# Second product of an FFN as seven products of half blocks in place of eight, after attention, on one core

## Chip, core and metric

One core of a Trainium2 chip. The metric is the device time of one execution in microseconds (us). The kernel before takes 512.01 us (median of 3 runs, 511.5 to 512.92). Positions in the timeline are counted from the start of the profiler's span of one execution. PE is the matrix engine (PEld its loading of weights), DVE the vector engine, ACT the scalar engine, POOL the engine that issues the loads.

## Reference

Attention with projected keys and values (8 batches, 8 heads, 1024 tokens, head size 64), then a feed-forward network (FFN) whose hidden values are squared:

```python
k_proj, v_proj = einsum('ks,bhsd->bhkd', E, k), einsum('ks,bhsd->bhkd', F, v)
x = softmax(q @ k_proj.T / 8) @ v_proj        # heads joined: 8192 x 512
h = maximum(x @ w_in, 0.0)                    # 8192 x 2048
out = (h * h) @ w_out                         # 8192 x 512
```

## The kernel before

Each batch is cut into two chunks of 512 tokens. A chunk is 16 steps of the first product, then its second product. Attention for the next batch is put between these steps by hand (the `plan`).

```python
def square(self, c, fb, ps):                  # after each block of the first product
    r = relu_pool.tile([P, TCH], BF16, name="h_relu")
    nc.scalar.activation(r[:], ps[:], AF.Relu)
    nc.vector.tensor_tensor(out=self.hsq[c][:, fb, :], in0=r[:], in1=r[:], op=ALU.mult)

def first_mm(self, c, fb, cb, ps):            # 64 per chunk, 128x512
    nc.tensor.matmul(ps[:], lhsT=w_in_blk(cb, fb), rhs=..., ...)

def second_mm(self, c, tb, fb, ps, m=slice(0, DM)):    # 4 token blocks x 16 = 64 per chunk, 128x512
    nc.tensor.matmul(ps[:, m], lhsT=self.hsq[c][:, fb, tb * P:(tb + 1) * P], rhs=w_out_blk(fb)[:, m], ...)
...
with tc.manual_schedule(engines={PE}):        # only PE runs in the order of this text
    ...
    att.project_v(V_PIECES[0])
    ...
    for b in range(B):
        if b == 0:
            at(1, att.project_v, V_PIECES[1])           # PE, then a cast of vp on DVE
            at(2, att.chunk_values, 0, 1, (0,))         # PE reads vp; then xT on DVE
            at(2, att.project_v, V_PIECES[2])
            at(3, att.chunk_values, 0, 1, (1,))
            ...
```

Each engine but PE gets its order when the kernel is built, not from the text.

The softmax here doesn't subtract the row's maximum and nothing guards it: scores larger than these inputs give would overflow.

Of the kernel before, what the change touches and what calls it, by code (L numbers as in the profile page):

```python
# [8 lines left out]
P = 128  # L9
F32 = mybir.dt.float32  # L10
BF16 = mybir.dt.bfloat16
AF = mybir.ActivationFunctionType
ALU = mybir.AluOpType
# [5 lines left out]
def kernel(  # L19
# [11 lines left out]
    nc = tc.nc  # L31

    B, H, S, D = q.shape
# [3 lines left out]
    DM = moe_w_out.shape[1]  # L37
    assert D == 64 and KP == 64 and C == CM == 512 and S == 1024 and H == 8
    NI = 8
# [9 lines left out]


    out_rows = out.rearrange("(b p i) m -> b i p m", p=P, i=NI)

    const_pool = ctx.enter_context(tc.tile_pool(name="const", bufs=1))
    wpool = ctx.enter_context(tc.tile_pool(name="wpool", bufs=1))
    qkv_pool = ctx.enter_context(tc.tile_pool(name="qkv", bufs=2))
    proj_pool = ctx.enter_context(tc.tile_pool(name="proj", bufs=2))
    qt_pool = ctx.enter_context(tc.tile_pool(name="qt", bufs=2))
    soft_pool = ctx.enter_context(tc.tile_pool(name="soft", bufs=3))
    x_pool = ctx.enter_context(tc.tile_pool(name="x", bufs=2))
    relu_pool = ctx.enter_context(tc.tile_pool(name="relu", bufs=8))  # L60
    hsq_pool = ctx.enter_context(tc.tile_pool(name="hsq", bufs=2))
    out_pool = ctx.enter_context(tc.tile_pool(name="outp", bufs=4))
    aps = ctx.enter_context(tc.tile_pool(name="aps", bufs=2, space=bass.MemoryType.PSUM))
    fps = ctx.enter_context(tc.tile_pool(name="fps", bufs=4, space=bass.MemoryType.PSUM))
# [4 lines left out]
    def bank(shape=(P, 512), dtype=F32):  # L69
        return fps.tile(list(shape), dtype, tag="bank", name="ps_bank")  # L70
# [53 lines left out]
    for j in range(WP):  # L124
        if j == WP - 1:
            load(Q0[:, :, 4:8, :], tokens(q, 0, i=slice(4, 8)))
        t = wpool.tile([P, fn, DM], BF16, name=f"w_out_{j}")
        load(t[:], w_out_view[:, j * fn:(j + 1) * fn, :])
        w_out_sb.append(t)

    def w_in_blk(cb, fb):
        t, j = w_in_at[fb]
# [2 lines left out]
    def w_out_blk(fb):  # L135
        return w_out_sb[fb // fn][:, fb % fn, :]
# [214 lines left out]
    class Ffn:  # L351
# [6 lines left out]
        def square(self, c, fb, ps):  # L358
            r = relu_pool.tile([P, TCH], BF16, name="h_relu")
            nc.scalar.activation(r[:], ps[:], AF.Relu)  # L360
            nc.vector.tensor_tensor(out=self.hsq[c][:, fb, :], in0=r[:], in1=r[:], op=ALU.mult)  # L361

        def first_mm(self, c, fb, cb, ps):
            nc.tensor.matmul(  # L364
# [3 lines left out]

        def second_mm(self, c, tb, fb, ps, m=slice(0, DM)):
            nc.tensor.matmul(  # L370
                ps[:, m], lhsT=self.hsq[c][:, fb, tb * P:(tb + 1) * P], rhs=w_out_blk(fb)[:, m],
                start=(fb == 0), stop=(fb == NFB - 1),
            )

# [5 lines left out]

        def steps(self):
            for c in range(2):
                self.hsq[c] = hsq_pool.tile([P, NFB, TCH], BF16, name="hsq")
                first = self.cold and c == 0
                fb0 = 0
                if first:

                    banks = [bank() for _ in range(4)]
                    for cbs, fbs in (
                        ((0, 1), (0, 1)), ((0, 1), (2, 3)), ((2,), (0, 1)), ((2,), (2, 3)), ((3,), (0, 1, 2, 3)),  # L390
                    ):
                        for fb in fbs:
                            for cb in cbs:
                                self.first_mm(c, fb, cb, banks[fb])
                            if cbs[-1] == NCB - 1:
                                self.square(c, fb, banks[fb])
                        if (cbs, fbs) != ((2,), (2, 3)):
                            yield
                    fb0 = 4
                for fb in range(fb0, NFB):  # L400
                    ps = bank()
                    for cb in range(NCB):
                        self.first_mm(c, fb, cb, ps)
                    self.square(c, fb, ps)
                    yield
                if first:

                    for t0 in range(0, 4, 2):
                        banks = [bank() for _ in range(2)]
                        for j in range(WP):  # L410
                            for t in range(2):
                                for fb in range(j * fn, (j + 1) * fn):
                                    self.second_mm(c, t0 + t, fb, banks[t])
                                if j == WP - 1:
                                    self.store(c, t0 + t, banks[t])
                                yield
                else:
                    last = self.b == B - 1 and c == 1
                    for tb in range(4):
                        if last and tb == 3:  # L420

                            for m in (slice(0, DM // 2), slice(DM // 2, DM)):
                                ps = bank()
                                for fb in range(NFB):
                                    self.second_mm(c, tb, fb, ps, m)
                                self.store(c, tb, ps, m)
                            break
                        ps = bank()
                        for j in range(WP):
                            for fb in range(j * fn, (j + 1) * fn):  # L430
                                self.second_mm(c, tb, fb, ps)
                            if j == WP - 1:
                                self.store(c, tb, ps)
                            yield

    with tc.manual_schedule(engines={PE}):
# [29 lines left out]
        for b in range(B):  # L466
            plan = {}

            def at(step, fn, *args, **kwargs):
                plan.setdefault(step, []).append(lambda: fn(*args, **kwargs))  # L470

            if b == 0:
                at(1, att.project_v, V_PIECES[1])
                at(2, att.chunk_values, 0, 1, (0,))
                at(2, att.project_v, V_PIECES[2])
                at(3, att.chunk_values, 0, 1, (1,))
                at(21, att.transpose_q_chunk, 1, Q0, 0)
                at(21, att.transpose_q_chunk, 1, Q0, 1)
                at(23, att.chunk_scores, 1, 0)
                at(23, att.chunk_scores, 1, 1)  # L480
                at(25, att.sums, 0)
                at(27, att.chunk_values, 1, 0)
                at(27, att.chunk_values, 1, 1)
                nxt = Attention(1)
                nxt.load()
            if b + 1 < B:
                if b + 2 < B:
                    coming = Attention(b + 2)
                    coming.load()
                if b == 0:  # L490
                    at(36, nxt.project)
                    at(39, nxt.transpose_q, 0)
                    at(39, nxt.transpose_q, 1)
                    at(39, nxt.transpose_k)
                    at(41, nxt.scores, 0)
                    at(41, nxt.scores, 1)
                    at(44, nxt.transpose_q, 2)
                    at(44, nxt.transpose_q, 3)
                    at(45, nxt.sums, 0)
                    at(48, nxt.values, 0, True)  # L500
                    at(48, nxt.scores, 2)
                    at(51, nxt.values, 1)
                    at(51, nxt.scores, 3)
                    at(55, nxt.sums, 2)
                    at(55, nxt.values, 2)
                    at(55, nxt.values, 3, True)
                else:
                    at(14, nxt.scores, 0)
                    at(14, nxt.scores, 1)
                    at(18, nxt.sums, 0)  # L510
                    at(18, nxt.values, 0, True)
                    at(18, nxt.scores, 2)
                    at(27, nxt.values, 1)
                    at(27, nxt.scores, 3)
                    at(49, nxt.sums, 2)
                    at(49, nxt.values, 2)
                    at(49, nxt.values, 3, True)
                if b + 2 < B:
                    if b == 0:
                        at(61, coming.project)  # L520
                        at(63, coming.transpose_q_dma)
                        at(64, coming.transpose_k)
                    else:
                        at(27, coming.project)
                        at(30, coming.transpose_q_dma)
                        at(29, coming.transpose_k_dma)
            for step, _ in enumerate(Ffn(att, b == 0).steps(), 1):
                for stage in plan.pop(step, []):
                    stage()
            assert not plan, plan  # L530
            att, nxt = nxt, coming
# [30 lines left out]
```

## Time and profile before

| | before |
|---|---|
| time, us | 512.01 |
| PE busy | 97% |
| a batch in the steady part (first chunk + second chunk), us | 31.80 + 28.63 = 60.43 |
| first chunk of the last batch, without attention, us | 27.63 |
| start of the second batch's FFN, us | 90.35 |

The head of the profile page: busy time of each engine, its share of the span, and its instructions.

```profile
span 511.2 us, 6930 instructions
...
PE 498.3 (97%) x2727; PEld 223.3 (44%) x2778; DVE 217.0 (42%) x438; ACT 273.2 (53%) x412; POOL 33.0 (6%) x45
...
PEclk9999999999999999999999999999999999999999
```

PE is busy throughout, at full clock (a 9 stands for 90% or more). The view of PE's waits (who waited for whom: total us, times, longest; `issue` means for nothing that the profile shows) has nothing large:

```profile
PE ps_bank L370 <- issue: 2.9, 18, 0.2
PE ps_bank L151 <- DVE zeros L107: 1.2, 1, 1.2
PE ps_bank L364 <- ACT o_sb L377: 1.1, 2, 0.8
...
```

The timeline of PE (start us, us, line, result and operands, shape, count; in brackets the idle time before and what ended it). L364 is the first product, L370 the second:

```profile
212.65 1.89 PE L364 MATMUL ps_bank<-xT,w_in_115 128*128 128x512 bf16 x8
...
244.45 1.89 PE L364 MATMUL ps_bank<-xT,w_in_115 128*128 128x512 bf16 x8
...
273.08 1.24 PE L364 MATMUL ps_bank<-xT,w_in_115 128*128 128x512 bf16 x5
...
452.52 1.89 PE L364 MATMUL ps_bank<-xT,w_in_115 128*128 128x512 bf16 x8
...
480.15 1.03 PE L364 MATMUL ps_bank<-xT,w_in_115 128*128 128x512 bf16 x4
...
502.59 1.03 PE L370 MATMUL ps_bank<-w_out_131,hsq 128*128 128x512 bf16 x4
503.46 1.03 PE L370 MATMUL ps_bank<-w_out_134,hsq 128*128 128x512 bf16 x4
504.32 0.60 PE L370 MATMUL ps_bank<-w_out_127,hsq 128*128 128x256 bf16 x4
504.76 0.60 PE L370 MATMUL ps_bank<-w_out_129,hsq 128*128 128x256 bf16 x4
```

The first five lines are the starts of chunks: three of the steady part give 31.80 and 28.63 us, and the two of the last batch 27.63 us. The others give the price of a matmul from start to start: 0.863 us for four of 512 columns, 215.8 ns each, and 0.4375 us for four of 256, 109.4 ns each. Durations overlap, so starts are to be read, not durations.

Last, the same view for PE in the start (L211 projects v, L272 uses the result `vp`, L364 is the FFN):

```profile
19.85 0.64 PE L211 MATMUL ps_att<-V_sb,FT 128*64 128x128 bf16 x16
20.52 1.04 PE L364 MATMUL ps_bank<-xT,w_in_118 128*128 128x512 bf16 x4
21.49 0.30 PE L272 MATMUL ps_att<-expT,vp 64*64 64x256 bf16 x4
21.78 0.64 PE L211 MATMUL ps_att<-V_sb,FT 128*64 128x128 bf16 x16
```

### The profile page before, as it was taken

How to read it: one execution, taken by the hardware profiler on the slowest of the kernel's cores; microseconds unless marked ns; L12 is line 12 of the kernel's file. 1: busy time of each engine (PE TensorE's matmuls, PEld its weight loads, DVE VectorE, ACT ScalarE, POOL GpSimd, SP SyncE). 2: the span in 40 equal slices, each digit the busy share in tenths (PEclk: the TensorE clock that was granted, in tenths of full speed). 3: DMA queues.
4: the chain of work that ended last, by engine and by line, in shares of the span. 5: the costliest groups of instructions: out<-in, count | busy, mean ns of one | idle time of the engine just before them, and what ended most of it. 6: DMA issues, size and time to landing. Idle time of an engine off the chain costs nothing.

```text
span 511.2 us, 6930 instructions
## 1 busy us (share of the span) xinstructions
PE 498.3 (97%) x2727; PEld 223.3 (44%) x2778; DVE 217.0 (42%) x438; ACT 273.2 (53%) x412; POOL 33.0 (6%) x45
## 2 busy tenths in 40 slices
PE   8899999999999999999999999999999999999997
PEld 4344444444444444444444444444444444444444
DVE  2453766444434445345352354434443443522130
ACT  2464584664717556375654837366472755544351
POOL 7420100121000020001000000000000000000000
PEclk9999999999999999999999999999999999999999
DMA  9999999899997199204931060100102011010102
GB/s 179 204 205 223 225 207 205 129 232 181 185 203 157 42 176 206 82 0 115 184 82 44 1 161 16 61 22 32 62 1 81 2 42 42 23 61 21 63 0 82
DMA packets 67872, 54.18 MB, mean 106 GB/s; under 512 B 29184, under 2 KB 59392, under 8 KB 67840
## 3 DMA queue, kind: packets, MB, share of 16 engines
q0 software_dynamic: 30640, 29.23, 36.3%
q1 hardware_dynamic: 37200, 24.52, 18.0%
q8 instruction: 21, 0.34, 0.3%
q14 instruction: 11, 0.09, 0.1%
HBM read 59.24 MB, written 16.78 MB: 149 GB/s over the span
## 4 chain that ended last, share of the span: by engine, by line
PE 85%; DMA 9%; issue 2%; ACT 2%; POOL 1%; DVE 1%; SPq 0%; POOLq 0%; ACTq 0%
PE ps_bank L364 40%; PE ps_bank L370 38%; DMA w_out_134<-in_moe_w_out_dram 4%; DMA V_sb<-in_v_dram 3%; PE ps_bank L191 2%; DMA out_dram<-o_sb 2%; PE ps_att L262 1%; PE ps_att L296 1%; PE ps_att L318 1%; PE ps_bank L318 1%; DVE rs L306 1%; ACT rs L301 0%; ACT rs L300 0%; PE ps_bank L247 0%; ACT expT L276 0%
## 5 line engine op out<-in xcount | busy, mean ns | idle before, releaser
L361 DVE TENSOR_TENSOR hsq<-h_relu 128x512 bf16<-128x512 bf16 x256 | 108.9, 425 | 192.9 <-ACT h_relu L360 191.8
L360 ACT ACTIVATE h_relu<-ps_bank 128x512 bf16<-128x512 f32 x256 | 151.3, 599 | 69.7 <-PE ps_bank L364 69.6
L370 PEld LDWEIGHTS <-hsq 128*128 128x128 bf16 x1040 | 99.7, 98 | 123.5 <-issue 9.3
L377 ACT COPY o_sb<-ps_bank 128x512 f32<-128x512 f32 (+1 forms) x65 | 37.7, 580 | 121.2 <-PE ps_bank L370 111.4
L370 PE MATMUL ps_bank<-w_out_127,hsq 128*128 128x512 bf16 (+1 forms) x257 | 65.6, 376 | 0.2
L370 PE MATMUL ps_bank<-w_out_134,hsq 128*128 128x512 bf16 (+1 forms) x251 | 64.1, 376 | 1.6 <-issue 1.1
L370 PE MATMUL ps_bank<-w_out_131,hsq 128*128 128x512 bf16 (+1 forms) x252 | 64.3, 376 | 1.1 <-issue 1.0
L370 PE MATMUL ps_bank<-w_out_129,hsq 128*128 128x512 bf16 (+1 forms) x249 | 64.2, 376 | 1.1 <-issue 0.8
L306 DVE COPY rs<-rs 32x1024 f32<-32x1024 f32 x60 | 41.6, 693 | 47.0 <-ACT rs L301 46.0
L364 PE MATMUL ps_bank<-xT,w_in_125 128*128 128x512 bf16 x255 | 59.0, 379 | 0.1
L364 PE MATMUL ps_bank<-xT,w_in_121 128*128 128x512 bf16 x250 | 57.7, 379 | 0.4
L364 PE MATMUL ps_bank<-xT,w_in_123 128*128 128x512 bf16 x247 | 57.4, 379 | 0.4
L276 ACT ACTIVATE expT<-ps_att 128x1024 bf16<-128x1024 f32 x32 | 31.8, 1023 | 18.0 <-PE ps_att L262 18.0
L364 PEld LDWEIGHTS <-w_in_123 128*128 128x128 bf16 x256 | 25.0, 98 | 30.4 <-issue 0.4
L364 PEld LDWEIGHTS <-w_in_121 128*128 128x128 bf16 x256 | 24.9, 98 | 30.3 <-issue 0.7
L364 PEld LDWEIGHTS <-w_in_125 128*128 128x128 bf16 x256 | 24.4, 98 | 31.0 <-issue 2.7
L364 PE MATMUL ps_bank<-xT,w_in_115 128*128 128x512 bf16 x128 | 30.9, 379 | 1.1 <-DVE xT L347 1.1
L364 PE MATMUL ps_bank<-xT,w_in_118 128*128 128x512 bf16 x126 | 30.3, 379 | 1.3 <-ACT o_sb L377 1.1
L300 ACT ACTIVATE rs<-ps_att 128x1024 f32<-128x1024 f32 x15 | 15.4, 1024 | 12.7 <-PE ps_att L296 12.7
L322 DVE TENSOR_TENSOR xT<-ps_att,rs 128x512 bf16<-128x512 f32 x28 | 18.1, 686 | 8.8 <-PE ps_att L318 8.5
L364 PEld LDWEIGHTS <-w_in_115 128*128 128x128 bf16 x128 | 12.5, 98 | 16.5 <-issue 2.3
L364 PEld LDWEIGHTS <-w_in_118 128*128 128x128 bf16 x128 | 12.3, 98 | 16.4 <-issue 1.7
(72 smaller groups left out, 237.1 us busy)
## 6 DMA issues: line engine op xcount, KB each, us to landing
out_dram<-o_sb SPq DMA_DIRECT2D x63, 256.0 KB, 2.0
K_sb<-in_k_dram POOLq DMA_DIRECT2D x7, 1024.0 KB, 22.1
V_sb<-in_v_dram POOLq DMA_DIRECT2D x7, 1024.0 KB, 26.8
Q_sb<-in_q_dram POOLq DMA_DIRECT2D x7, 1024.0 KB, 14.8
k_f_93<-in_k_dram SPq DMA_DIRECT2D x1, 512.0 KB, 4.2
Q_sb<-in_q_dram POOLq DMA_DIRECT2D x2, 256.0 KB, 7.2
K_sb<-in_k_dram POOLq DMA_DIRECT2D x1, 512.0 KB, 7.9
V_sb<-in_v_dram POOLq DMA_DIRECT2D x1, 512.0 KB, 10.1
```

The source lines that it names most:

```text
L191: nc.tensor.matmul(ps[LO, :], lhsT=ET[:, i, :], rhs=self.K[:, :, i, :], start=f, stop=l)
L262: nc.tensor.matmul(ps[o, par], lhsT=self.kT[r, h % 4, h // 4, :], rhs=self.qT[r, h, n, :], start=True, stop=True)
L276: nc.scalar.activation(e[:], ps[:], AF.Exp, scale=SCALE)
L300: nc.scalar.activation(rs[1][:], ps[:], AF.Ln)
L306: nc.vector.tensor_copy(rs[j][lack:lack + 32], rs[j][have:have + 32])
L318: nc.tensor.matmul(ps_x[par][o], lhsT=self.vp[r, 2 * pr + a, :], rhs=e[r, par], start=True, stop=True)
L322: nc.vector.tensor_tensor(out=self.xT[:, pr, :, par], in0=ps_x[par].rearrange("p (c t) -> p c t", c=2), in1=rs[:, par].rearrange("p (c t) ...
L360: nc.scalar.activation(r[:], ps[:], AF.Relu)
L361: nc.vector.tensor_tensor(out=self.hsq[c][:, fb, :], in0=r[:], in1=r[:], op=ALU.mult)
L364: nc.tensor.matmul(ps[:], lhsT=w_in_blk(cb, fb), rhs=self.xT[:, cb, c].rearrange("p a t -> p (a t)"), start=(cb == 0), stop=(cb == NCB - 1),)
L370: nc.tensor.matmul(ps[:, m], lhsT=self.hsq[c][:, fb, tb * P:(tb + 1) * P], rhs=w_out_blk(fb)[:, m], start=(fb == 0), stop=(fb == NFB - 1),)
L377: nc.scalar.copy(o[:, m], ps[:, m])
```

## The change

It cuts a chunk's h into quarters (two halves of tokens, two of the hidden size) and w_out likewise, and forms the product of two 2x2 block matrices with seven block products in place of eight (a scheme after Strassen and Winograd). The price is sums of quarters: of h once per chunk, of w_out once. It is used from the second batch on. Pools shrink to make room. Two smaller parts are not shown below: the last token block is no longer split into halves of 256 columns, and some attention steps no longer use spare banks.

```diff
-    qt_pool = ctx.enter_context(tc.tile_pool(name="qt", bufs=2))
+    qt_pool = ctx.enter_context(tc.tile_pool(name="qt", bufs=1))
-    relu_pool = ctx.enter_context(tc.tile_pool(name="relu", bufs=8))
+    relu_pool = ctx.enter_context(tc.tile_pool(name="relu", bufs=4))
...
+    w_sum = wpool.tile([P, 4, HF, HM], BF16, name="w_sum")
+    def sum_w_out():                          # 8 DVE instructions, 128x1024 bf16
+        for j in range(2):
+            ...
+            for o, x, y in ((t1, b12, b11), (t3, b22, b12), (t2, b22, t1), (t4, b21, t2)):
+                nc.vector.tensor_tensor(out=o, in0=x, in1=y, op=ALU.subtract)
...
+        def sum_h(self, c, f):                # 4 DVE instructions, twice per chunk
+            ...
+        def half_product(self, c, n, i, ps, fresh):
+            h = self.h_form(c, n)
+            for fb in range(HF):              # 8 matmuls, 128x256
+                nc.tensor.matmul(ps[:, i * HM:(i + 1) * HM], lhsT=h[:, fb, i * P:(i + 1) * P],
+                                 rhs=w_out_form(n, fb), ...)
...
+        def seven_products(self, c):
+            first, chain, other = bank(), bank(), bank()
+            half(c, 1, 0, first, True)
+            yield
+            half(c, 1, 1, first, True)
+            nc.scalar.copy(chain[:], first[:])
+            ...                               # 5, 6, 2, 7, 2, 4, 3; chain copied out to u after 6 and 7
...
-                for fb in range(fb0, NFB):
+                order = [fb for j in range(HF) for fb in (j, HF + j)] if seven else range(fb0, NFB)
+                for n, fb in enumerate(order):
...
-                    at(18, nxt.scores, 2)
+                    at(21, nxt.scores, 2)     # and 27 -> 26, 49 -> 48, 49 -> 51 for other steps
...
                     if b == 0:
                         at(61, coming.project)
                         at(63, coming.transpose_q_dma)
                         at(64, coming.transpose_k)
+                        at(64, sum_w_out)     # the last step of the first batch
```

More of the change, by code (lines that the diff above doesn't have):

```diff
@@ L51 @@
     out_rows = out.rearrange("(b p i) m -> b i p m", p=P, i=NI)
+    out_tokens = out.rearrange("(b p i) m -> b p i m", p=P, i=NI)
+    HF, HM = NFB // 2, DM // 2
     const_pool = ctx.enter_context(tc.tile_pool(name="const", bufs=1))
@@ L56 @@
     proj_pool = ctx.enter_context(tc.tile_pool(name="proj", bufs=2))
-    qt_pool = ctx.enter_context(tc.tile_pool(name="qt", bufs=2))
+    qt_pool = ctx.enter_context(tc.tile_pool(name="qt", bufs=1))
     soft_pool = ctx.enter_context(tc.tile_pool(name="soft", bufs=3))
     x_pool = ctx.enter_context(tc.tile_pool(name="x", bufs=2))
-    relu_pool = ctx.enter_context(tc.tile_pool(name="relu", bufs=8))
+    relu_pool = ctx.enter_context(tc.tile_pool(name="relu", bufs=4))
     hsq_pool = ctx.enter_context(tc.tile_pool(name="hsq", bufs=2))
+    form_pool = ctx.enter_context(tc.tile_pool(name="form", bufs=1))
+    part_pool = ctx.enter_context(tc.tile_pool(name="part", bufs=2))
     out_pool = ctx.enter_context(tc.tile_pool(name="outp", bufs=4))
@@ L129, with w_out_form @@
         w_out_sb.append(t)
+    w_sum = wpool.tile([P, 4, HF, HM], BF16, name="w_sum")
+    def sum_w_out():
+        for j in range(2):
+            f = slice(j * fn, (j + 1) * fn)
+            t1, t2, t3, t4 = (w_sum[:, n, f] for n in range(4))
+            up, down = w_out_sb[j], w_out_sb[j + 2]
+            b11, b12, b21, b22 = up[:, :, 0:HM], up[:, :, HM:DM], down[:, :, 0:HM], down[:, :, HM:DM]
+            for o, x, y in ((t1, b12, b11), (t3, b22, b12), (t2, b22, t1), (t4, b21, t2)):
+                nc.vector.tensor_tensor(out=o, in0=x, in1=y, op=ALU.subtract)
+    def w_out_form(n, fb):
+        return {
+            1: lambda: w_out_blk(fb)[:, 0:HM], 2: lambda: w_out_blk(HF + fb)[:, 0:HM],
+            3: lambda: w_out_blk(HF + fb)[:, HM:DM], 4: lambda: w_sum[:, 3, fb], 5: lambda: w_sum[:, 0, fb],
+            6: lambda: w_sum[:, 1, fb], 7: lambda: w_sum[:, 2, fb],
+        }[n]()
     def w_in_blk(cb, fb):
@@ L360, in square, with quarter @@
             nc.scalar.activation(r[:], ps[:], AF.Relu)
-            nc.vector.tensor_tensor(out=self.hsq[c][:, fb, :], in0=r[:], in1=r[:], op=ALU.mult)
+            rv = r.rearrange("p (a t) -> p a t", a=2)
+            nc.vector.tensor_tensor(out=self.hsq[c][:, fb // HF, :, fb % HF, :], in0=rv, in1=rv, op=ALU.mult)
+        def quarter(self, c, kh, a):
+            return self.hsq[c][:, kh, a]
+        def sum_h(self, c, f):
+            a11, a12, a21, a22 = (self.quarter(c, kh, a)[:, f] for a in range(2) for kh in range(2))
+            s1, s2, s4 = (self.h_sum[:, n, f] for n in range(3))
+            for o, x, op, y in (
+                (s1, a21, ALU.add, a22), (s2, s1, ALU.subtract, a11),
+                (a21, a11, ALU.subtract, a21), (s4, a12, ALU.subtract, s2),
+            ):
+                nc.vector.tensor_tensor(out=o, in0=x, in1=y, op=op)
@@ new lines, in h_form @@
+        def h_form(self, c, n):
+            return {
+                1: lambda: self.quarter(c, 0, 0), 2: lambda: self.quarter(c, 1, 0), 3: lambda: self.h_sum[:, 2],
+                4: lambda: self.quarter(c, 1, 1), 5: lambda: self.h_sum[:, 0], 6: lambda: self.h_sum[:, 1],
+                7: lambda: self.quarter(c, 0, 1),
+            }[n]()
+        def half_product(self, c, n, i, ps, fresh):
+            h = self.h_form(c, n)
+            for fb in range(HF):
+                nc.tensor.matmul(
+                    ps[:, i * HM:(i + 1) * HM], lhsT=h[:, fb, i * P:(i + 1) * P], rhs=w_out_form(n, fb),
+                    start=fresh and i == 0 and fb == 0, stop=fb == HF - 1, skip_group_check=True,
+                )
@@ new lines, in put, with keep @@
+        def put(self, c, a, mh, ps, more=None):
+            o = out_pool.tile([P, DM], F32, name="o_sb")
+            if more is None:
+                nc.scalar.copy(o[:], ps[:])
+            else:
+                nc.vector.tensor_tensor(out=o[:], in0=ps[:], in1=more[:], op=ALU.add)
+            nc.sync.dma_start(
+                out_tokens[self.b][:, 4 * c + a:4 * c + a + 3:2, mh * HM:(mh + 1) * HM],
+                o.rearrange("p (i m) -> p i m", i=2),
+            )
+        def keep(self, ps):
+            u = part_pool.tile([P, DM], F32, name="u")
+            nc.scalar.copy(u[:], ps[:])
+            return u
@@ new lines, in seven_products @@
+        def seven_products(self, c):
+            first, chain, other = bank(), bank(), bank()
+            half = self.half_product
+            half(c, 1, 0, first, True)
+            yield
+            half(c, 1, 1, first, True)
+            nc.scalar.copy(chain[:], first[:])
+            yield
+            half(c, 5, 0, other, True)
+            yield
+            half(c, 5, 1, other, True)
+            yield
+            half(c, 6, 0, chain, False)
+            yield
+            half(c, 6, 1, chain, False)
+            u2 = self.keep(chain)
+            yield
+            half(c, 2, 0, first, False)
+            yield
+            half(c, 7, 0, chain, False)
+            yield
+            half(c, 7, 1, chain, False)
+            u3 = self.keep(chain)
+            yield
+            half(c, 2, 1, first, False)
+            self.put(c, 0, 0, first)
+            self.put(c, 1, 1, other, u3)
+            yield
+            half(c, 4, 0, chain, False)
+            yield
+            half(c, 4, 1, chain, False)
+            self.put(c, 1, 0, chain)
+            yield
+            half(c, 3, 0, other, False)
+            yield
+            half(c, 3, 1, other, False)
+            self.put(c, 0, 1, other, u2)
+            yield
@@ L370, in second_mm @@
             nc.tensor.matmul(
-                ps[:, m], lhsT=self.hsq[c][:, fb, tb * P:(tb + 1) * P], rhs=w_out_blk(fb)[:, m],
+                ps[:, m], lhsT=self.quarter(c, fb // HF, tb // 2)[:, fb % HF, (tb % 2) * P:(tb % 2 + 1) * P],
+                rhs=w_out_blk(fb)[:, m],
                 start=(fb == 0), stop=(fb == NFB - 1),
@@ L382, in steps @@
             for c in range(2):
-                self.hsq[c] = hsq_pool.tile([P, NFB, TCH], BF16, name="hsq")
+                self.hsq[c] = hsq_pool.tile([P, 2, 2, HF, HC], BF16, name="hsq")
+                seven = self.b > 0
+                if seven:
+                    self.h_sum = form_pool.tile([P, 3, HF, HC], BF16, name="h_sum")
                 first = self.cold and c == 0
@@ L404, in steps @@
                     self.square(c, fb, ps)
+                    if seven and n % HF == HF - 1:
+                        self.sum_h(c, slice(n // HF * HF // 2, (n // HF + 1) * HF // 2))
                     yield
@@ L416, in steps @@
                                 yield
+                elif seven:
+                    yield from self.seven_products(c)
                 else:
-                    last = self.b == B - 1 and c == 1
                     for tb in range(4):
-                        if last and tb == 3:
-                            for m in (slice(0, DM // 2), slice(DM // 2, DM)):
-                                ps = bank()
-                                for fb in range(NFB):
-                                    self.second_mm(c, tb, fb, ps, m)
-                                self.store(c, tb, ps, m)
-                            break
                         ps = bank()
@@ L510 @@
                     at(18, nxt.sums, 0)
-                    at(18, nxt.values, 0, True)
-                    at(18, nxt.scores, 2)
-                    at(27, nxt.values, 1)
-                    at(27, nxt.scores, 3)
-                    at(49, nxt.sums, 2)
-                    at(49, nxt.values, 2)
-                    at(49, nxt.values, 3, True)
+                    at(18, nxt.values, 0)
+                    at(21, nxt.scores, 2)
+                    at(26, nxt.values, 1)
+                    at(26, nxt.scores, 3)
+                    at(48, nxt.sums, 2)
+                    at(48, nxt.values, 2)
+                    at(51, nxt.values, 3)
                 if b + 2 < B:
@@ L522 @@
                         at(64, coming.transpose_k)
+                        at(64, sum_w_out)
                     else:
-                        at(27, coming.project)
+                        at(26, coming.project)
                         at(30, coming.transpose_q_dma)
-                        at(29, coming.transpose_k_dma)
+                        at(28, coming.transpose_k_dma)
             for step, _ in enumerate(Ffn(att, b == 0).steps(), 1):
```

## The prediction

> **What bounds the kernel.** The matrix engine (PE). The profile page shows PE busy 498.3 of 511.2 us at granted clock 1.0, ACT 53%, DVE 42%. The view of waits gives PE about 8 us of waits. From the second batch on the timeline repeats every 60.4 us, with 128x512 matmuls spaced 215.8 ns apart (four in 0.863 us).
>
> **What it removes.** One chunk's second product is 64 matmuls of 512 columns: 13.81 us. The new form is 7 products x 2 token blocks x 8 = 112 matmuls of 256 columns. The last 32 matmuls of before have that form, each with its own weight load: the timeline shows four in 0.4375 us, 109.4 ns each. The Trainium skill ("TensorE: Matmul & The Clock Gate", Back-to-back issue gap) gives N/2.4 + 2.5 ns, 109.2 for 256; the trace agrees. 112 x 109.4 = 12.25 us, 1.56 us less per chunk, 14 chunks: **21.8 us** off PE, all critical.
>
> **What it adds (per chunk).**
> - DVE: 8 sums of 128x1024 bf16. The trace has 128x512 bf16 at 425 ns, which fits (150 + N/2)/0.96 from "VectorE: DVE Perf Modes" (Side-by-side); estimate 690 ns each, 5.5 us. Two 128x512 f32 adds out of PSUM, like the xT multiply (686 ns): 1.4 us. DVE rises from 26.4 to about 40 of 60 us per batch: no bound.
> - ACT: one 586 ns copy more. Neutral.
> - Once: 8 sums of w_out, 5.5 us on DVE as batch 1 starts; four banks and four relu buffers cover about 6.9 us of PE.
>
> **Where new waits can come.**
> 1. Product 1 needs h block 7, squared second last, 0.77 us after the first product's end. In first chunks with attention, two exponentials (1.93 us on ACT) put that square at about +1.15 us: 0.5 us stall, x6 = 3 us. Second chunks: none.
> 2. ACT copies `chain` out twice per chunk; PE has 0.87 us of other work to hide a 0.59 us copy plus latency. Only where the third scores' exponential (1.02 us) is ahead does it show: 0.25 x 6 = 1.5 us.
> 3. Two more insertions of attention matmuls per batch, about 0.3 us of spacing each: 3.6 us.
> 4. Tail: the last 256-column copy (372 ns) becomes a 690 ns add: +0.4. Start of batch 1: +0.5.
> 5. The stall before batch 2 (1.1 us, output copies waiting for stores stuck behind a transpose) should go: -1.
>
> Sum: 512.0 - 21.8 + 3 + 1.5 + 3.6 + 0.9 - 1 = 498.2; I say **498 us**, range 492 to 503. Faster by over 2% (below 501.8): 0.83; within 2%: 0.16; slower: 0.01.
>
> **What would show each step.** 14 x 112 second-product matmuls of 256 columns at 109-110 ns; PE busy near 478; the period near 58.5 us with attention, 52 for the last batch (55.3 before). DVE groups of h sums near 690 ns, x112. PE waits: for DVE hsq before the first half product, for ACT "u" copies before half products into `chain`, none above 1 us.
>
> **What would make it wrong.** 256-column matmuls that don't sustain 109 ns in the stream (at 125 ns most of the gain is gone); ACT or DVE order putting exponentials, inversions (3 us) or sums (2.8 us) ahead of what PE waits for, 1-2 us per chunk; one bank left while three are held; four relu buffers blocking behind the sums.

## More of the kernel before

PE hands v to DVE and gets `vp` back within a microsecond. In DVE's timeline, the cast between the two stands here:

```profile
20.53 0.29 DVE L214 CAST vp<-ps_att 128x128 bf16<-128x128 f32 x1 [1.47 <-PE ps_att L211]
```

## The result

The kernel after takes 511.73 us (median of 4 runs, 511.56 to 511.92), beside 512.10 us for before. The ratio is 0.9987, with a 95% interval of 0.9969 to 1.0006: no change. (A ratio here is the mean time of one kernel's fast runs over that of the other's of the same rounds, so it is not quite the ratio of the medians quoted.) The record holds no check of its result; e1_late below, which differs only in an order on DVE, was correct. The predicted 498 us, with its range of 492 to 503, was wrong.

The head of the page after:

```profile
span 510.1 us, 8489 instructions
...
PE 487.1 (96%) x3434; PEld 287.8 (56%) x3434; DVE 304.9 (60%) x586; ACT 282.7 (55%) x425; POOL 32.5 (6%) x45
...
PEclk9958999999999999999999999999999999999999
```

PE's share hardly moved, but the clock line has a hole, a 5 and an 8 near 25 to 50 us. PE's waits say what stands there:

```profile
PE ps_att L296 <- DVE vp L238: 12.4, 2, 11.2
PE ps_bank L471 <- DVE xT L371: 2.0, 3, 1.5
PE ps_bank L410 <- DVE hsq L386: 1.9, 6, 0.3
```

The timeline of PE after (L410 is a half product, L471 the first product, L477 the second product of the first batch, L296 uses `vp`, L235 projects v):

```profile
20.23 0.64 PE L235 MATMUL ps_att<-V_sb,FT 128*64 128x128 bf16 x16
20.80 1.04 PE L471 MATMUL ps_bank<-xT,w_in 128*128 128x512 bf16 x4
33.08 0.43 PE L296 MATMUL ps_att<-expT,vp 64*64 64x256 bf16 x4 [11.24 <-DVE vp L238]
33.43 1.07 PE L235 MATMUL ps_att<-V_sb,FT 128*64 128x128 bf16 x16
35.98 1.01 PE L471 MATMUL ps_bank<-xT,w_in 128*128 128x512 bf16 x2 [1.48 <-DVE xT L371]
38.13 0.43 PE L296 MATMUL ps_att<-expT,vp 64*64 64x256 bf16 x4 [1.13 <-DVE vp L238]
...
106.45 1.89 PE L471 MATMUL ps_bank<-xT,w_in 128*128 128x512 bf16 x8
...
222.87 12.25 PE L471 MATMUL ps_bank<-xT,w_in 128*128 128x512 bf16 x56
...
253.81 13.98 PE L471 MATMUL ps_bank<-xT,w_in 128*128 128x512 bf16 x64
...
281.08 2.10 PE L471 MATMUL ps_bank<-xT,w_in 128*128 128x512 bf16 x9
...
453.86 0.81 PE L471 MATMUL ps_bank<-xT,w_in 128*128 128x512 bf16 x3
...
479.91 1.46 PE L471 MATMUL ps_bank<-xT,w_in 128*128 128x512 bf16 x6
...
493.72 1.91 PE L410 MATMUL ps_bank<-w_out,hsq 128*128 128x256 bf16 x16
495.47 3.66 PE L410 MATMUL ps_bank<-w_sum,h_sum 128*128 128x256 bf16 x32
```

Both halves of the story are in these lines. From 222.87 on, the chunks last 30.94 and 27.27 us in place of 31.80 and 28.63, and 16 half-block matmuls take 495.47 - 493.72 = 1.75 us, 109.4 ns each: the seven products deliver. But at about 21.8 us, where before went on at once, PE stops for 11.24 us, twice more for over a microsecond, and the second batch starts at 106.45 in place of 90.35 us.

| us | before | after | difference |
|---|---|---|---|
| start to second batch | 90.35 | 106.45 | +16.10 |
| second batch to end of span | 420.89 | 403.64 | -17.25 |

What PE waited for is to be seen in DVE's timeline after:

```profile
18.14 1.29 DVE L371 TENSOR_TENSOR xT<-ps_att,rs 128x512 bf16<-128x512 f32 x2 [0.60 <-PE ps_att L296]
32.13 0.69 DVE L146 TENSOR_TENSOR w_sum<-w_out 128x1024 bf16<-128x1024 bf16 x1 [12.69 <-DMA w_out<-in_moe_w_out_dram]
32.74 0.28 DVE L238 CAST vp<-ps_att 128x128 bf16<-128x128 f32 x1
34.63 0.69 DVE L146 TENSOR_TENSOR w_sum<-w_out 128x1024 bf16<-128x1024 bf16 x1 [1.61 <-DMA w_out<-in_moe_w_out_dram]
35.24 0.68 DVE L371 TENSOR_TENSOR xT<-ps_att,rs 128x512 bf16<-128x512 f32 x1
```

L146 is the sum of w_out. The text has it at step 64 of the first batch. The build put its first part between the first `xT` multiplies and the `vp` cast, where DVE came to it at about 19.4 us, and the others among the instructions that follow. DVE then sat idle for 12.69 us, waiting for a load, with a 0.28 us cast behind it whose input was ready at about 20.9 us. The Trainium skill ("TensorE: Matmul & The Clock Gate", Part 1, the paragraph Engine queue depths) says that the vector engine's queue is strictly first in, first out; this trace agrees: the cast ran at 32.74 us, right behind the sum.

The idle stretch also costs clock. Busy time by stretch (stretch, us, then each engine, then PEclk):

```profile
28.00:33.00 5.00, 0.00 (x0) 0.00 (x0) 0.87 (x2) 0.00 (x0) 1.35 (x3) 0.50 1.24 206
...
43.00:45.00 2.00, 2.00 (x11) 0.94 (x10) 2.00 (x7) 1.47 (x3) 0.00 (x0) 1.00 1.25 209
```

The clock was 0.50 from about 25.7 to 42.8 us. The skill (same page, Part 1: The HAM clock gate) states half rate after an idle window of about 3.4 us and release after about as much sustained work; here it fell about 4 us after the last matmuls and came back about 4 us after 38.5, when dense work began again. The three waits above sum to 13.85 us of the 16.1; most of the rest is probably matmuls at half clock (an estimate from this trace: half of the dense stretch from 38.5 to 42.8 us, about 2.1 us).

### The profile page after: what moved, and what is told of

The parts are those of the page before. It is cut to its first block, busy times and chain, and to the rows that moved or that the text cites. A ratio compares the mean times of both kernels' runs of the same rounds, so it can differ in the third digit from the quotient of the medians.

```text
span 510.1 us, 8489 instructions
## 1 busy us (share of the span) xinstructions
PE 487.1 (96%) x3434; PEld 287.8 (56%) x3434; DVE 304.9 (60%) x586; ACT 282.7 (55%) x425; POOL 32.5 (6%) x45
## 4 chain that ended last, share of the span: by engine, by line
PE 86%; DMA 6%; issue 3%; ACT 3%; DVE 1%; POOL 1%; POOLq 0%
PE ps_bank L471 41%; PE ps_bank L410 33%; PE ps_bank L477 4%; DMA w_out<-in_moe_w_out_dram 3%; DMA V_sb<-in_v_dram 3%; PE ps_bank L215 2%; PE ps_att L342 2%; ACT h_relu L384 1%; PE ps_att L320 1%; PE ps_att L286 1%; ACT expT L300 1%; DVE hsq L386 1%; DVE xT L371 0%; PE ps_bank L271 0%; POOL K_sb L80 0%
## 5 line engine op out<-in xcount | busy, mean ns | idle before, releaser
L471 PE MATMUL ps_bank<-xT,w_in 128*128 128x512 bf16 x1024 | 228.8, 382 | 2.1 <-DVE xT L371 2.0
L471 PEld LDWEIGHTS <-w_in 128*128 128x128 bf16 x1024 | 99.6, 98 | 122.8 <-issue 9.7
L410 PEld LDWEIGHTS <-hsq 128*128 128x128 bf16 x896 | 86.6, 98 | 19.0 <-DVE hsq L386 3.6
L410 PEld LDWEIGHTS <-h_sum 128*128 128x128 bf16 x672 | 63.8, 98 | 12.5 <-issue 5.5
L410 PE MATMUL ps_bank<-w_out,hsq 128*128 128x256 bf16 x448 | 56.8, 273 | 1.9 <-DVE hsq L386 1.9
L410 PE MATMUL ps_bank<-w_sum,hsq 128*128 128x256 bf16 x448 | 53.5, 273 | 0.0
L410 PE MATMUL ps_bank<-w_sum,h_sum 128*128 128x256 bf16 x448 | 53.4, 273 | 0.0
L330 DVE COPY rs<-rs 32x1024 f32<-32x1024 f32 x60 | 41.1, 685 | 20.3 <-ACT rs L325 19.4
L420 DVE TENSOR_TENSOR o_sb<-ps_bank,u 128x512 f32<-128x512 f32 x28 | 19.4, 691 | 46.9 <-PE ps_bank L410 30.4
L477 PE MATMUL ps_bank<-w_out,hsq 128*128 128x512 bf16 x128 | 29.2, 380 | 0.0
L410 PE MATMUL ps_bank<-w_out,h_sum 128*128 128x256 bf16 x224 | 26.7, 273 | 0.0
L477 PEld LDWEIGHTS <-hsq 128*128 128x128 bf16 x128 | 11.9, 98 | 15.5 <-issue 1.9
L398 DVE TENSOR_TENSOR h_sum<-hsq 128x1024 bf16<-128x1024 bf16 x28 | 19.4, 692 | 1.0
## 6 DMA issues: line engine op xcount, KB each, us to landing
V_sb<-in_v_dram POOLq DMA_DIRECT2D x7, 1024.0 KB, 19.4
Q_sb<-in_q_dram POOLq DMA_DIRECT2D x7, 1024.0 KB, 15.2
```

Of the source, the lines that this page charges most:

```text
L330: nc.vector.tensor_copy(rs[j][lack:lack + 32], rs[j][have:have + 32])
L398: nc.vector.tensor_tensor(out=o, in0=x, in1=y, op=op)
L410: nc.tensor.matmul(ps[:, i * HM:(i + 1) * HM], lhsT=h[:, fb, i * P:(i + 1) * P], rhs=w_out_form(n, fb), start=fresh and i == 0 and fb == 0 ...
L420: nc.vector.tensor_tensor(out=o[:], in0=ps[:], in1=more[:], op=ALU.add)
L471: nc.tensor.matmul(ps[:], lhsT=w_in_blk(cb, fb), rhs=self.xT[:, cb, c].rearrange("p a t -> p (a t)"), start=(cb == 0), stop=(cb == NCB - 1),)
L477: nc.tensor.matmul(ps[:, m], lhsT=self.quarter(c, fb // HF, tb // 2)[:, fb % HF, (tb % 2) * P:(tb % 2 + 1) * P], rhs=w_out_blk(fb)[:, m], ...
```

## The experiments

The theory after this reading: the sums of w_out, early in DVE's queue, waited for the w_out loads and held up `vp`. Rivals: (A) the smaller pools slow the first batch; (B) the seven products are no gain; (C) the work of the sums in the start, not their wait, costs the time. The first four runs shared a chip; e5 to e7 ran on another, where before took 512.46 us beside 512.30. So their differences from e1_late go across chips, and the lengths of batches in the traces are the safer measure.

### e1_late: the sums held back

The sums get an order-only edge (the build must place one instruction behind another, though no data passes between them): none may stand on DVE before the last square of the first batch.

```diff
-            nc.vector.tensor_tensor(out=self.hsq[c][:, fb // HF, :, fb % HF, :], in0=rv, in1=rv, op=ALU.mult)
+            last_square[0] = nc.vector.tensor_tensor(out=self.hsq[c][:, fb // HF, :, fb % HF, :], in0=rv, ...)
...
     def sum_w_out():
+        with tc.issue_after(last_square[0].ins):
+            sum_w_out_now()
```

> Same kernel as after, but the eight w_out sums may not stand on the vector engine before the last square of the first batch. Theory (the sums stood ahead of the early casts of vp in the vector engine's in-order queue and waited there for the w_out loads): the 11.2 us wait of PE for vp goes, batch 1 starts near 90 us in place of 106.5, and the time is 90.3 + 403.7 = 494 to 497 us. Rival A (fewer q and relu buffers slow the first batch): the time stays at 509 to 512. Rival B (256-column products are no gain in the steady part): also 508 or more.

Measured: 496.32 us, correct; ratio to before 0.969 (0.9676 to 0.9704). In its PE timeline the second batch starts at 90.73 us:

```profile
90.73 1.55 PE L477 MATMUL ps_bank<-xT,w_in 128*128 128x512 bf16 x5
```

Its list of PE waits, longest first, begins with another one and holds no `vp` any more:

```profile
PE ps_bank L416 <- DVE hsq L392: 1.9, 6, 0.3
...
```

One order edge, with no other change in the work, takes 15.4 us off the median; the first sum now starts at 77.30 us, when the loads have landed. A and B fall as causes of the loss.

### e2_before_sums: the sums alone, on the kernel before

Eight-block products as before, the two smaller pools, and the sums added with their result unused. They take the same places in DVE's queue as in after.

```diff
...
+                        at(64, sum_w_out)
```

> The kernel before, with its eight-block products, plus only the eight w_out sums (result unused) and the two smaller pools. The sums stand in the same places of the vector engine's queue as in after. Theory: it loses what after lost at the start, about 16 us: 526 to 530 us, with the same wait of 11 us of PE for vp. Rival (the loss comes from the seven products): 511 to 513.

Measured: 526.95 us, correct; ratio 1.0294 (1.0276 to 1.0312). The same wait, somewhat shorter, is in its list:

```profile
PE ps_att L284 <- DVE vp L226: 10.5, 2, 9.4
```

So the loss of the start comes without the seven products: 526.95 - 511.76 (e3, below) = 15.2 us.

### e3_before_pools: the pools alone

```diff
-    qt_pool = ctx.enter_context(tc.tile_pool(name="qt", bufs=2))
+    qt_pool = ctx.enter_context(tc.tile_pool(name="qt", bufs=1))
-    relu_pool = ctx.enter_context(tc.tile_pool(name="relu", bufs=8))
+    relu_pool = ctx.enter_context(tc.tile_pool(name="relu", bufs=4))
```

> The kernel before with one q buffer in place of two and four relu buffers in place of eight, nothing else. Theory: 511 to 513 us, no wait of PE over 1.5 us. Rival A (the smaller pools cost the first batch): 515 to 528 us.

Measured: 511.76 us; ratio 0.9994 (0.9979 to 1.0008). The pools cost nothing that shows, at most 0.1% by the interval. Rival A is refuted by itself, too.

### e4_ready: the sums early, but on data that is there

After, with the eight sums tied behind the first `xT` multiplies, reading part of k in place of w_out. Its output is wrong, which doesn't matter for the time.

```diff
+        with tc.issue_after(first_x[0].ins):
+            sum_ready()
...
+        ready = K0[:, 4:6].rearrange("p h i d -> p (h i d)").rearrange("p (f m) -> p f m", m=HM)
+            for o, x, y in ((t1, ready, ready), (t3, ready, ready), (t2, ready, t1), (t4, ready, t2)):
```

> After, with the eight sums in the same early place of the queue but reading data that has long arrived (part of k; the result is wrong on purpose). It tells the wait for the load from the work of the sums. Theory (it is the wait): vp is late by at most the length of four sums, 2.8 us; batch 1 starts 1 to 4 us later than in before; 495 to 499 us. Rival C (the 5.5 us of vector work in the start, or its traffic, is what costs): 505 to 511 us.

Measured: 496.68 us; ratio 0.9699 (0.9681 to 0.9717). DVE's timeline in the start:

```profile
19.46 1.29 DVE L385 TENSOR_TENSOR xT<-ps_att,rs 128x512 bf16<-128x512 f32 x2 [0.60 <-PE ps_att L310]
20.66 1.28 DVE L151 TENSOR_TENSOR w_sum<-K_sb 128x1024 bf16<-128x1024 bf16 x2
21.86 0.69 DVE L151 TENSOR_TENSOR w_sum<-K_sb,w_sum 128x1024 bf16<-128x1024 bf16 x1
22.46 0.28 DVE L252 CAST vp<-ps_att 128x128 bf16<-128x128 f32 x1
```

Sums of the same size stand ahead of the same cast (three here, one in after), and the time is within 0.4 us of e1_late's. The order was harmful only because the sums waited for data: in after, four of the eight did, 16.9 us in all. Rival C falls.

### e5_order: the wait for block 7

This run tests the first wait that the prediction named. The second eight h blocks are made in another order, so that block 7, the last one that product 1 needs, is squared three blocks earlier (12th of 16 and no longer 15th; the expectation's "five" is a miscount). Base: e1_late.

```diff
-                order = [fb for j in range(HF) for fb in (j, HF + j)] if seven else range(fb0, NFB)
+                order = (0, 8, 1, 9, 2, 10, 3, 11, 4, 5, 6, 7, 12, 13, 14, 15) if seven else range(fb0, NFB)
```

> e1_late with the second eight h blocks of each chunk in the order 4 5 6 7 12 13 14 15, so that block 7, which product 1 needs last, is squared five blocks earlier. Theory (the six waits of 0.32 us for hsq in first chunks are that block): the waits go, the first chunks last 30.6 in place of 30.93 us, and the time falls by about 2 us, to 494.3. Rival (the wait is for the vector engine's sums or for something else): the period stays 30.93 and the time 496.3.

Measured: 493.75 us, correct; ratio 0.9635 (0.9614 to 0.9655). Product 1 of a first chunk in after:

```profile
295.55 0.93 PE L410 MATMUL ps_bank<-w_out,hsq 128*128 128x256 bf16 x7
296.80 1.16 PE L410 MATMUL ps_bank<-w_out,hsq 128*128 128x256 bf16 x9 [0.32 <-DVE hsq L386]
```

and in e5_order:

```profile
221.40 1.91 PE L416 MATMUL ps_bank<-w_out,hsq 128*128 128x256 bf16 x16
```

The wait is gone. A whole batch lasts 57.72 us in place of 58.21 in e1_late, 0.49 less; six batches make 2.9, and the time fell by 2.57. The idle of 0.32 us that the list of waits shows is less than what the wait cost: the seventh matmul started at about 295.55 + 6 x 0.109 = 296.21 and the eighth at 296.80, a gap of 0.59 where 0.11 is the rule, so 0.48 us was lost. The difference is the overlap of durations: the seventh matmul's 0.27 us last until 296.48, and only what comes after counts as idle. The expectation's 30.6 us came from the 0.32; it is best checked over whole batches, because in this trace the first matmuls of some chunks are missing, which moves the border between chunks by 0.22 us.

### e6_early: the first batch's second chunk, too

Base: e5_order. The sums stand behind the last `xT` multiply near 53 us, and the second chunk of the first batch uses seven products. Three more steps of attention move one or two places earlier.

```diff
-                seven = self.b > 0
+                seven = self.b > 0 or c == 1
...
-                    at(55, nxt.values, 3, True)
+                    at(58, nxt.values, 3)
...
-                        at(64, sum_w_out)
+                        at(28, sum_w_out)
```

> e5_order with seven products in the second chunk of the first batch too: the sums of w_out are held behind the last xT multiply of the first batch's second chunk (near 53 us), when w_out has landed, and one value step of attention moves from step 55 to 58. Arithmetic on PE alone: 1.4 to 1.6 us less, 492.8. Against it: the vector engine is nearly full from 54 to 92 us in e1_late, and has 11 us more to do before 92 us; if that binds, 494 to 497.

Measured: 495.71 us, correct; ratio 0.9675 (0.9653 to 0.9697): 2.0 us worse than e5_order. PE now waits for DVE in the first batch:

```profile
PE ps_bank L417 <- DVE xT L352: 1.9, 1, 1.9
...
PE ps_bank L417 <- ACT u L435: 0.4, 1, 0.4
```

DVE is busy 32.1 of the 38 us from 54 to 92 us, against 29.1 in e5_order. That a full DVE is the cause fits the listed waits, but they sum to less than the loss (1.5 us not gained and 2.0 us lost), so the rest stays open, and the moved steps are a rival that was not tested.

### e7_split: one more place where attention interrupts the FFN

Base: e1_late. It measures what an added insertion of attention matmuls (one more place where they stand between those of the FFN) costs.

```diff
-                    at(26, nxt.scores, 3)
+                    at(27, nxt.scores, 3)
```

> e1_late with the fourth score step of attention moved from step 26 to 27, one more place per batch where attention matmuls stand between FFN matmuls (six batches). The prediction's claim of 0.3 us each: first chunks 31.2 us, time plus 1.8. From the second chunks (1.36 us gained of 1.56, with one place more and no wait): 0.2 us each, first chunks 31.13, plus 1.2 us. Rival (places cost nothing, the missing 0.2 us is something else): 30.93 and 496.3.

Measured: 497.74 us, correct; ratio 0.9715 (0.9695 to 0.9735), 1.42 us over e1_late. A batch lasts 58.44 us, 0.23 more. That is nearer to the 0.2 us read from the second chunks than to the 0.3 of the prediction.

## Why the prediction was wrong

The failing step is this one: "Once: 8 sums of w_out, 5.5 us on DVE as batch 1 starts; four banks and four relu buffers cover about 6.9 us of PE", entered in the sum as "Start of batch 1: +0.5". Its size of 5.5 us was right (eight at 690 ns). Its place was wrong: it was taken from the text, where the sums stand at step 64, and for DVE the text's order does not bind. The first of them stood at 19.4 us, ahead of the `vp` cast, and waited there for a load that ended at 32 us. The start of batch 1 came 16.1 us later, not 0.5. e1 (place alone), e2 (sums alone) and e4 (no wait) show it from three sides. "ACT or DVE order" was among what could go wrong, but sized at 1 to 2 us per chunk, with computing ahead of what PE needs; that an instruction waiting for a load could stand there was not thought of.

The other terms, in us, from the traces of before, after, e1, e5 and e7:

| term of the prediction | predicted | measured | read from |
|---|---|---|---|
| matmuls off PE, 14 chunks | -21.8 | -22.1 | last batch's first chunk 27.63 to 26.05, 1.58 x 14 |
| 1: wait for block 7 | +3 | +2.9 | e5: 0.49 x 6 |
| 2: copies of `chain` | +1.5 | 0 | no wait for `u` in the list of after |
| 3: 12 more insertions | +3.6 | +2.4 to 2.8 | second chunks 0.20; e7 0.23 |
| 4: tail | +0.4 | +0.7 | last matmul's end to span's end, 3.26 and 3.93 (e1) |
| 4: start of batch 1 | +0.5 | **+16.1** | 90.35 to 106.45 |
| 5: stall before batch 2 | -1 | -1.4 | that period was 61.87 in before; see below |
| sum | -13.8 | -1.4 to -1.0 | spans: 511.24 to 510.09 |

Term 5 is not shown to be a gain of the change. The stall stands in one trace of before, whose span of 511.2 us is at the top of what that kernel's other runs show (509.5 to 511.2); e3_before_pools, without the seven products, has no such stall (60.43 us).

The mechanism that the prediction rested on, 112 matmuls of 256 columns at 109 ns in place of 64 at 216, held to within 2%. For the skill's back-to-back formula, spacings of 215.8 and 109.4 ns agree with its 215.8 and 109.2; for the bf16 time on the vector engine, 684 to 692 ns measured agree with the 690 estimated from the figures of "VectorE: DVE Perf Modes" (Side-by-side). With the sums in the place that the prediction assumed, e1_late's 496.32 us lies in its range, 1.9 us under the predicted sum of 498.2; terms 2 and 3 were set 2.3 to 2.7 us too high.

## What to carry to other kernels

Work that is emitted late is not late where the build orders an engine's queue: look up where it stands in each in-order queue, above all an instruction whose only input is a load: it blocks all that stands behind it until the load lands. Why the build placed it so early was not looked into; that it looked free to go first is a guess. Tie such work behind an instruction that comes after the landing. And when a change moves a time by nothing, take the span apart by stage before doubting the mechanism: here -17 and +16 us lay side by side.

## What the Trainium skill lacked or had wrong

- "TensorE: Matmul & The Clock Gate", Back-to-back issue gap, gives about 131 ns per matmul of N=512 for a sustained stream of weight load and matmul pairs, and calls N/2.4 + 2.5 ns the gap of an isolated one that over-counts. The sustained stream ran at 215.8 ns for 512 columns and 109.4 ns for 256, with a 98 ns weight load per matmul: the isolated formula is the right one here. The point is about that section alone: Part 1 of the page gives the same formula for back-to-back matmuls.
- The same page, Engine queue depths, states the strict order of the vector engine's queue, but not what it can cost: here 12.69 us of one instruction's wait for a load held a 0.28 us cast, and with it PE for 11.24 us.
- No page that was used says that an idle time listed ahead of a matmul understates the loss: 0.32 us idle was listed where about 0.48 us between starts was lost.
